# The second layer's gate and value products by Strassen's seven-product form

## The chip, the cores and the metric

The kernel runs on one core of a Trainium2 chip. Times are device microseconds (us) of that core. TensorE (PE in the rows) multiplies, VectorE (DVE), ScalarE (ACT) and GpSimd (POOL) do the elementwise work, SyncE (SP) starts the transfers. SBUF holds the tiles; PSUM holds the sums of the matmuls in eight banks of 128 x 512 fp32, which ScalarE and VectorE can read and write too.

## What is computed

Three layers follow each other, for 4 x 576 = 2304 tokens of 512 features:

```python
x = softmax(q k^T / 8 + decay, causal) v            # 32 heads of 64; heads side by side give x: 2304 x 512
h = x @ w_in;  x = (h * tanh(softplus(h))) @ w_out  # first layer, 512 -> 2048 -> 512
gate = 1 / (1 + exp(-(x @ w_gate)))                 # second layer, 512 -> 1536
out  = (gate * (x @ w_val)) @ w_out2                # 1536 -> 512
```

The weights come as float64.

## The kernel before

Every fp32 product is made of three fp16 products: an operand is split in a high part and the rest (`scaled` writes the high part, `rest` the low one), and `high*high + high*low + low*high` is accumulated in PSUM. A weight tile of 128 x 512 comes in as float64 by one DMA (`load_w`, L536); three VectorE instructions (L558, L562, L566) make fp32 of it, then high part and rest are written.

**Order of the work.** The instructions are not written in program order. Each piece of work is a Python generator that yields what it wants next (an engine and an estimated duration, a key, a buffer). `Order` (L33) runs them all on estimated clocks and issues, engine by engine, what can start first, by due time among those ready. A wrong estimate changes no result, only the order on the five engines. `AFTER` is the estimated delay between the end of an instruction and the start of another that needs it. Every engine then works through its own list in order and waits at the head of it.

**First layer.** Steps of 256 tokens by 256 hidden features (72 of them). `h_stream` makes x @ w_in in a PSUM tile, `mish` puts the activation through ScalarE and VectorE into `g` (L827, L833, L837), `y_stream` multiplies with w_out some steps later, `y_out` writes the new x (`xt`) back in its high and low parts (L919, L921).

**Second layer.** Blocks of 512 tokens (`XB`: four of 512, the last of 256) by steps of 128 hidden features, 60 steps. `gv_stream` (L957 to L978) makes, for each step, the gate in one PSUM tile and the value in another: for each, 4 parts of the 512 input features x 3 matmuls, each with 512 token columns (256 in the last block): 24 matmuls a step. `glu` (L981) takes the gate through ScalarE's tanh (L989), multiplies with the value on VectorE (L992) and splits the result into `zz`. `o_stream` (L1005) multiplies `zz` with w_out2 (3 matmuls of 512 columns for each 128 tokens of a step) and accumulates over the 12 steps of a block in four PSUM tiles; `store` writes them out. `w2_stream` (L934) starts the 36 loads of these weights, spread over the steps of the first layer from step 56 on.

Of the kernel before, what the change touches and what calls it, by code (L numbers as in the profile page):

```python
# [7 lines left out]
FP32 = mybir.dt.float32  # L8
FP16 = mybir.dt.float16
BF16 = mybir.dt.bfloat16  # L10
I32 = mybir.dt.int32
# [13 lines left out]
S_VL = 2.0 ** 4  # L25
# [4 lines left out]
S_Z = S_Y * S_VL * 2.0  # L30
# [21 lines left out]
class Order:  # L52
# [29 lines left out]
    def spawn(self, gen, due):  # L82
        self.n += 1
        t = {"time": self.cur["time"] if self.cur else 0.0, "due": due, "n": self.n, "gen": gen}
        self.step(t, None)

    def step(self, t, value):
        outer, self.cur = self.cur, t
        last = t.get("req", ("",))[0]
# [5 lines left out]
        if r and last == r[0] == "PE":  # L95
            t["time"] -= self.AFTER["PE"]
        if r is None:
            return
        if r[0] in self.ops:
            self.ops[r[0]].append(t)  # L100
        else:
            self.blocked.append(t)
            self.changed = True

# [3 lines left out]
    def done(self, *keys):  # L108
        for k in keys:
            self.event[k] = self.cur["time"]  # L110
        self.changed = True

    def give(self, tag, i):
        self.freed[tag][i] = self.cur["time"]
        self.changed = True

    def pick(self, *plans):

        now, due = self.cur["time"], self.cur["due"]
# [82 lines left out]
    def run(self):  # L202
        while True:
# [29 lines left out]
            if dma:  # L233
# [6 lines left out]
                else:  # L240
                    t["time"] = end
            else:
# [30 lines left out]
def attention_moe_moe_kernel(ctx, tc, qk, v, f, rows_q, rows_k, w_in, w_out, w_gate, w_val, w_out2, out):  # L273
# [26 lines left out]
        "d": 2, "r": 2, "g": 4, "pq": 2,  # L300
        "sp": 4, "pp": 3, "pt": 5, "stage": 4, "vt": 4, "sm": 6, "low": 2, "q": NQ,
        "wr": 3, "wf": 2, "wr2": 2, "wf2": 2,
# [69 lines left out]
    def decay():  # L372
# [3 lines left out]
        zt = mt.tile([128, 768], FP32, tag="pq", name="zt", bufs=BUFS["pq"])[0:NH, 0:S + 1]  # L376
        yield from take("pq")
# [24 lines left out]
        give("pq", 0)  # L402
# [133 lines left out]
    def load_w(hi, lo, src, scale, pool, key, n):  # L536
        wr, wf = ("wr", "wf") if pool is at else ("wr2", "wf2")
        if pool is at:

            yield from need(*(((("st", NPB - 1),),) + (("rq", "rk"),) * n)[n])  # L540
        (ri,) = yield from take(wr, turn=(wr, n))
        if pool is at:

            raw = words(xt[2 + (ri % 3 == 0)], ri % 3 // 2 * 2048, 2048).bitcast(I32)
            raw = raw.rearrange("p (n t) -> p n t", t=2)
        else:
            raw = pool.tile([128, 512, 2], I32, tag="wr", name="wraw", bufs=2)
        yield "SP", 0.5, 128 * 4096
        nc.sync.dma_start(
            out=raw.rearrange("p n t -> p (n t)").rearrange("p (a n) -> p a n", a=src.shape[1]), in_=src  # L550
        )
        (fi,) = yield from take(wf, turn=(wf, n))
        if pool is at:
            w = words(xt[4], fi % 2 * 1024, 1024).bitcast(I32)
        else:
            w = pool.tile([128, 512], I32, tag="wf", name="wf", bufs=2)
# [12 lines left out]
        give(wr, ri)  # L569
# [5 lines left out]
        give(wf, fi)  # L575
        done(key)

    def cols(t, w64, g, scale, pool, key):
# [3 lines left out]
                t[:, 0, k:k + 2], t[:, 1, k:k + 2], src[:, k:k + 2], scale, pool, ("w", key, g, k // 2), n  # L582
# [4 lines left out]
    def rows(t, w64, g, scale, pool, key):  # L587
# [4 lines left out]
                scale, pool, ("w", key, g, a), n,  # L592
# [249 lines left out]
    def h_stream():  # L842
        for i, (blk, g) in enumerate(steps1):
# [10 lines left out]
            for ff in range(2):  # L854
                dst = hp[:, ff * 256:ff * 256 + 256]
                for k in range(KD):
# [9 lines left out]
                    nc.tensor.matmul(dst, lhsT=wl, rhs=xh, start=False, stop=(k == KD - 1))  # L866
            spawn(mish(i, hp, tag, hi), i - MISH)
        done("h")

    def y_stream():  # L870
        for i, (blk, g) in enumerate(steps1):
# [8 lines left out]
            for dm in range(4):  # L880
# [17 lines left out]
                if end and dm % 2:  # L898
                    spawn(y_out(blk, half, acc, ai, g), -100)
            give("g", gi)  # L900
# [26 lines left out]
    w2, z_t = {}, {}  # L927
    W2DUE = 10
    W2BEG = 56
    W2GAP = 0.6  # L930
    NF2 = F2 // 128
    steps = [(blk, fi) for blk in range(len(XB)) for fi in range(NF2)]

    def w2_stream():  # L934
# [229 lines left out]
```

## Time and profile before

| | us |
|---|---|
| median of 3 runs (lowest, highest) | 977.32 (976.13, 978.79) |
| the profiled execution | 978.56 |
| its span, first to last instruction | 976.8 |
| TensorE busy | 914.6 (94%) |
| VectorE busy | 533.0 (55%) |
| ScalarE busy | 464.2 (48%) |
| GpSimd busy | 70.0 (7%) |
| mean granted TensorE clock | 0.993 of full speed |

The busy time of an engine is the union of its instructions' times. A matmul's record is longer than its share of the engine, since matmuls overlap: the time between the starts of two neighbours is what one costs when nothing waits. The chain that ended last is 84% TensorE.

### The profile page before, as it was taken

To read this page: it belongs to the slowest core of one execution; us is meant where nothing else is said; L and a number is where in the kernel's file an instruction comes from. 1 tells how busy PE (TensorE), PEld (TensorE's weight loads), DVE (VectorE), ACT (ScalarE), POOL (GpSimd) and SP (SyncE) were. 2 spreads that over 40 slices of the span, in tenths; PEclk is the share of its full clock that TensorE was granted. 3 is DMA by queue.
4 is the path that set the end of the run, shared out by engine and by line. 5 is a ranking of instruction groups with operands and counts; after the bars stand their busy time and mean duration, and the time that the engine had idled before them with its cause. 6 is when DMAs were issued, how large, how long until landed. Compare 5 with 4: busy or idle time off the path is not lost.

```text
span 976.8 us, 18268 instructions
## 1 busy us (share of the span) xinstructions
PE 914.6 (94%) x7368; PEld 608.9 (62%) x7368; DVE 533.0 (55%) x1262; ACT 464.2 (48%) x912; POOL 70.0 (7%) x74
## 2 busy tenths in 40 slices
PE   2377789999999999999999999999999999999998
PEld 1255568778888888788888744444444444444576
DVE  8998979875656647664888872222222222222232
ACT  8678769898787868886444431110001000100011
POOL 0211301112111102010000000000000000000000
PEclk9998999999999999999999999999999999999999
DMA  7697997668447745545455540010001000100010
GB/s 235 161 212 185 222 229 196 135 133 165 109 102 136 141 98 118 113 78 98 150 161 152 163 130 0 1 44 1 1 1 44 1 0 1 44 1 1 5 40 22
DMA packets 153546, 93.43 MB, mean 96 GB/s; under 512 B 109578, under 2 KB 135242, under 8 KB 153456
## 3 DMA queue, kind: packets, MB, share of 16 engines
q1 hardware_dynamic: 153462, 92.27, 39.2%
q8 instruction: 57, 0.93, 0.4%
q14 instruction: 27, 0.22, 0.1%
HBM read 50.71 MB, written 4.83 MB: 57 GB/s over the span
## 4 chain that ended last, share of the span: by engine, by line
PE 84%; DVE 9%; DMA 3%; issue 1%; SPq 1%; ACT 1%; POOL 0%; DVEq 0%; ACTq 0%; POOLq 0%
PE gv_ps L975 10%; PE gv_ps L976 10%; PE gv_ps L977 10%; PE y_ps L895 6%; PE y_ps L896 6%; PE y_ps L897 6%; PE h_ps L864 6%; PE h_ps L866 5%; PE h_ps L865 5%; PE o_acc L1025 5%; PE o_acc L1023 5%; PE o_acc L1024 5%; PE o_ps L775 3%; DVE pp L437 2%; PE s_ps L657 1%; PE s_ps L658 1%
## 5 line engine op out<-in xcount | busy, mean ns | idle before, releaser
L992 DVE SCALAR_TENSOR_TENSOR z<-t,gv_ps 128x512 f32<-128x512 f32 (+1 forms) x60 | 38.0, 634 | 286.6 <-PE gv_ps L977 250.1
L989 ACT ACTIVATE t<-gv_ps 128x512 f32<-128x512 f32 (+1 forms) x60 | 33.2, 553 | 285.3 <-PE gv_ps L977 276.7
L864 PE MATMUL h_ps<-xt,win 128*128 128x256 f16 x576 | 159.2, 276 | 4.8 <-DVE g L837 3.7
L895 PE MATMUL y_ps<-g,wout 128*128 128x256 f16 x576 | 158.9, 276 | 4.7 <-ACT wout L418 4.7
L896 PE MATMUL y_ps<-g,wout 128*128 128x256 f16 x576 | 158.5, 275 | 3.9 <-DVE wout L437 3.0
L865 PE MATMUL h_ps<-xt,win 128*128 128x256 f16 x576 | 158.8, 276 | 3.1 <-DVE xt L799 2.9
L866 PE MATMUL h_ps<-xt,win 128*128 128x256 f16 x576 | 159.0, 276 | 0.0
L897 PE MATMUL y_ps<-g,wout 128*128 128x256 f16 x576 | 158.5, 275 | 0.0
L605 DVE CUSTOM_DVE_ANT_0 sp<-s_ps,mask 128x384 f32<-128x384 f32 (+4 forms) x144 | 67.3, 494 | 36.9 <-PE s_ps L658 33.9
L976 PE MATMUL gv_ps<-xt,wg 128*128 128x512 f16 (+1 forms) x240 | 85.9, 358 | 0.0
L975 PE MATMUL gv_ps<-xt,wg 128*128 128x512 f16 (+1 forms) x240 | 85.9, 358 | 0.0
L977 PE MATMUL gv_ps<-xt,wg 128*128 128x512 f16 (+1 forms) x240 | 85.9, 358 | 0.0
L977 PE MATMUL gv_ps<-xt,wv 128*128 128x512 f16 (+1 forms) x240 | 85.9, 358 | 0.0
L975 PE MATMUL gv_ps<-xt,wv 128*128 128x512 f16 (+1 forms) x240 | 85.8, 358 | 0.0
L976 PE MATMUL gv_ps<-xt,wv 128*128 128x512 f16 (+1 forms) x240 | 85.8, 358 | 0.0
L437 DVE SCALAR_TENSOR_TENSOR pp<-sp,sm,pp 128x512 f16<-128x512 f32 (+4 forms) x120 | 75.1, 644 | 16.2 <-ACT pp L418 13.6
L1023 PE MATMUL o_acc<-wo,zz 128*128 128x512 f16 x216 | 81.9, 379 | 0.0
L1024 PE MATMUL o_acc<-wo,zz 128*128 128x512 f16 x216 | 81.9, 379 | 0.0
L1025 PE MATMUL o_acc<-wo,zz 128*128 128x512 f16 x216 | 81.9, 379 | 0.0
L673 ACT ACTIVATE sp<-sp,sm 128x384 f32<-128x384 f32 (+3 forms) x112 | 63.8, 570 | 19.6 <-DVE sm L605 19.1
L864 PEld LDWEIGHTS <-win 128*128 128x128 f16 x576 | 56.8, 99 | 18.1 <-issue 3.2
L418 ACT ACTIVATE pp<-sp,sm 128x384 f16<-128x384 f32 (+4 forms) x108 | 63.9, 608 | 8.0 <-DVE sm L630 3.3
(116 smaller groups left out, 1528.9 us busy)
## 6 DMA issues: line engine op xcount, KB each, us to landing
xt<-w_in SPq DMA_DIRECT2D x16, 512.0 KB
xt<-w_out SPq DMA_DIRECT2D x16, 512.0 KB
wraw<-w_gate SPq DMA_DIRECT2D x12, 512.0 KB
wraw<-w_val SPq DMA_DIRECT2D x12, 512.0 KB
wraw<-w_out SPq DMA_DIRECT2D x12, 512.0 KB
st<-qk SPq DMA_DIRECT2D x16, 320.0 KB
out<-ob SPq DMA_DIRECT2D x18, 256.0 KB
st<-qk SPq DMA_DIRECT2D x16, 256.0 KB
```

What stands on the lines that cost most here:

```text
L864: nc.tensor.matmul(dst, lhsT=wh, rhs=xh, start=(k == 0), stop=False)
L865: nc.tensor.matmul(dst, lhsT=wh, rhs=xl, start=False, stop=False)
L866: nc.tensor.matmul(dst, lhsT=wl, rhs=xh, start=False, stop=(k == KD - 1))
L895: nc.tensor.matmul(dst, lhsT=wh, rhs=gh, start=first, stop=False, skip_group_check=True)
L896: nc.tensor.matmul(dst, lhsT=wl, rhs=gh, start=False, stop=False, skip_group_check=True)
L897: nc.tensor.matmul(dst, lhsT=wh, rhs=gl, start=False, stop=last, skip_group_check=True)
L975: nc.tensor.matmul(dst, lhsT=wh, rhs=x[:, 0, k, :], start=(k == 0), stop=False)
L976: nc.tensor.matmul(dst, lhsT=wh, rhs=x[:, 1, k, :], start=False, stop=False)
L977: nc.tensor.matmul(dst, lhsT=wl, rhs=x[:, 0, k, :], start=False, stop=(k == KD - 1))
L1023: nc.tensor.matmul(dst, lhsT=zh, rhs=w[:, 0, ff, :], start=(fi == 0), stop=False)
L1024: nc.tensor.matmul(dst, lhsT=zh, rhs=w[:, 1, ff, :], start=False, stop=False)
L1025: nc.tensor.matmul(dst, lhsT=zl, rhs=w[:, 0, ff, :], start=False, stop=(fi == NF2 - 1))
```

## The change

**The product.** Two hidden steps (256 features) of a block now make one unit: 30 units, named u, of a block and a group j of 0 to 5. The 2 x 2 form is: x cut into token halves (first index) and feature halves (second index), A11, A12, A21, A22; the weights cut by feature halves of the input (rows) and into gate and value (columns): B11, B21 the gate's halves, B12, B22 the value's. Instead of eight products there are seven, in Winograd's arrangement with sums of x (`s`, made by `sums`) and sums of weights (`t1` to `t4`, made by `group`). Each product is 12 matmuls with half a block of columns (256, or 128 in the last block), where before a unit had 96/2 = 48 matmuls with a whole block of columns.

**The sums after the product.** Four PSUM banks A, B, C, D hold the running sums. After a product, ScalarE copies one bank to another (`copy`), and the next product accumulates onto the copy. In one unit TensorE does: b11 in A; t3 in D; t2 onto A; b21 onto B; t1 onto A; t4 onto C; b22 onto D. ScalarE copies A to B after b11, D to an SBUF tile e after t3, A to C after t2, A to D after t1. B is then the gate of the first token half, D its value; C + e is the gate of the second half, A + e its value, both added by VectorE. The output matmuls of the unit before stand in four slots between the products (`some`): after t3, b21, t4 and b22.

**The weights.** Each group takes six loads and three float64-to-fp32 instructions for each as before, then four sums and nine splits (before: six splits). Groups 0 to 2 have tiles of their own, groups 3 to 5 lie in the tiles of the first layer's weights that are free by then. The loads are no longer spread over steps by key; they start as buffers come free once attention is over.

**The order.** `Order` no longer adds the delay `AFTER` between two TensorE requests of one generator when there is a buffer or a key between them; it only adds it where another engine follows. This changes the order from the first layer's steps on. `zt`, a start-up tile, moves into an unused weight tile.

```diff
     def step(self, t, value):
         outer, self.cur = self.cur, t
-        last = t.get("req", ("",))[0]
...
-        if r and last == r[0] == "PE":
-            t["time"] -= self.AFTER["PE"]
...
         if r[0] in self.ops:
+            if r[0] != "PE":
+                t["time"] += t["lag"]
+            t["lag"] = 0.0
...
+            elif e == "PE":
+
+                t["time"], t["lag"] = end, self.AFTER[e]
...
+    def group(j, pool, n, where):
...
+        spawn(pair(w2["b11", j], f2[g1][0], S, ("w", "b11", j)), due)
+        yield from need(v1, ("w", "b11", j))
+        w_g1, w_v1 = f2[g1][0], f2[v1][0]
+        yield from mixed(w_g1, w_v1, w_g1)
+        split("t1", g1, S)
+        yield from need(v2)
+        w_v2 = f2[v2][0]
+        split("b22", v2, S_VL)
+        yield from add(w_v1, w_v2, w_v1, ALU.subtract, 512)
+        split("t3", v1, S_VL)
...
+        yield from mixed(w_v2, w_v2, w_g1)
...
+        split("t2", v2, S)
...
+        split("b21", g2, S)
...
+        yield from add(w_g2, w_g2, w_v2, ALU.subtract, 512)
...
+        split("t4", g2, S)
...
+    def sums(blk):
...
+        for q, fi in zip(("21", "22", "11", "12"), fis):
...
+            yield from add(w.rearrange("p (k n) -> p k n", k=2), part[0], part[1], ALU.add, n)
...
+                yield from add(f["22"][0], f["21"][0], f["22"][0], ALU.add, n)
+                spawn(s_pair(s[0], f["22"][0], n, ("s", blk, 1)), due)
...
+    def product(bank, piece, j, x, half, start):
...
+        for ff in range(2):
+            dst = bank[:, ff * half:ff * half + half]
+            yield "PE", t_pe(6, half)
+            for k in range(2):
...
+                nc.tensor.matmul(dst, lhsT=wh, rhs=xh[:, k], start=first, stop=False, skip_group_check=True)
+                nc.tensor.matmul(dst, lhsT=wh, rhs=xl[:, k], start=False, stop=False, skip_group_check=True)
+                nc.tensor.matmul(dst, lhsT=wl, rhs=xh[:, k], start=False, stop=last, skip_group_check=True)
+
+    def copy(dst, src, first, key):
+        yield from need(*first)
+        yield "ACT", t_act(dst.shape[1], 0.05)
+        nc.scalar.activation(out=dst, in_=src, func=ACTF.Copy)
+        done(key)
 
     def gv_stream():
         yield from need("h")
...
+        yield from take("h", "h", "h", "o")
+        banks = [t_ps(tag, f"bank{i}") for i, tag in enumerate(("h", "h", "h", "o"))]
+
+        yield "PE", t_pe(2, 512)
+        for t in banks[1:3]:
+            nc.tensor.matmul(t, lhsT=xt[0][:, 0, 0, 0:128], rhs=xt[0][:, 0, 1, :], start=True, stop=True)
...
+            yield from need(("v", u - 1), ("ad", u - 1))
+            yield from product(A, "b11", j, q["11"], half, True)
+            spawn(copy(B, A, [("t", u - 1)], ("ab", u)), -100)
+            yield from need(("z", u - 1), ("s", blk, 3))
+            yield from product(D, "t3", j, s[2], half, True)
...
+            spawn(copy(e, D, [], ("de", u)), -100)
+            yield from some(0)
+            yield from need(("ab", u), ("s", blk, 2))
+            yield from product(A, "t2", j, s[1], half, False)
+            spawn(copy(C, A, [("g", u - 1)], ("ac", u)), -100)
+            yield from product(B, "b21", j, q["12"], half, False)
...
+            yield from some(1)
+            yield from need(("ac", u), ("s", blk, 1))
+            yield from product(A, "t1", j, s[0], half, False)
+            spawn(copy(D, A, [("de", u)], ("ad", u)), -100)
...
+            yield from product(C, "t4", j, q["22"], half, False)
...
+            yield from some(2)
+            yield from need(("ad", u), ("s", blk, 4))
+            yield from product(D, "b22", j, s[3], half, False)
...
+    def second(u, v2, ri, C, e, ei, n):
...
+        nc.vector.tensor_tensor(e, C, e, op=ALU.add)
...
+        nc.scalar.activation(out=e, in_=e, func=ACTF.Tanh, scale=0.5 / (S_Y * S_GT))
...
+        nc.vector.scalar_tensor_tensor(v2, e, 1.0, v2, op0=ALU.add, op1=ALU.mult)
```

Where the instructions now stand is shown at three places. On TensorE, the first product of the second layer and what stands ahead of it, before (`gv_ps`, tile 8057; `y_ps` 7810 is the first layer's last block, with g of step 68):

```order
L896 MATMUL y_ps_7810<-g_7868,wout4_88 128x256
L897 LDWEIGHTS wout4_88
L897 MATMUL y_ps_7810<-g_7868,wout4_88 128x256
L975 LDWEIGHTS wg0_7020
L975 MATMUL gv_ps_8057<-xt0_71,wg0_7020 128x512
```

and now (`bank0` is A; `y_ps` with `g_7958` belongs to step 69; the y products of steps 70 and 71 stand behind the whole first unit):

```order
L899 MATMUL y_ps_7832<-g_7958,wout5_89 128x256
L900 LDWEIGHTS wout5_89
L900 MATMUL y_ps_7832<-g_7958,wout5_89 128x256
L1131 LDWEIGHTS b11_0_7018
L1131 MATMUL bank0_8125<-xt0_71,b11_0_7018 128x256
```

The second layer began after step 68's last y product and was mixed with the rest of them; it now begins after step 69's, with one product of 12 matmuls, and bank A is the PSUM tile that the last h step used.

On VectorE, the last g of the first layer (step 71) and what follows, before:

```order
L837 SCALAR_TENSOR_TENSOR g_8067<-h_ps_7992,g_8067 128x512
L437 SCALAR_TENSOR_TENSOR wg4_7031<-wf_8010,wg4_7031 128x512
L558 TENSOR_SCALAR wf_8059<-wraw_8037 128x512
L562 SCALAR_TENSOR_TENSOR wf_8059<-wraw_8037,wf_8059 128x512
L566 SCALAR_TENSOR_TENSOR wf_8059<-wraw_8037,wf_8059 128x512
```

and now:

```order
L838 SCALAR_TENSOR_TENSOR g_8092<-h_ps_8017,g_8092 128x512
L952 TENSOR_TENSOR wf_8006<-wf_8052,wf_8006 128x512
L544 TENSOR_SCALAR wf_8084<-wraw_8072 128x512
L958 SCALAR_TENSOR_TENSOR wout0_84<-wf_8052,wout0_84 128x512
L548 SCALAR_TENSOR_TENSOR wf_8084<-wraw_8072,wf_8084 128x512
L1052 SCALAR_TENSOR_TENSOR wf_8052<-wf_8052,wf_7970 128x512
L552 SCALAR_TENSOR_TENSOR wf_8084<-wraw_8072,wf_8084 128x512
```

Before, this g stood behind 24 of the 36 loads; now it stands behind 21, with their sums and splits (group 3's pieces go to `wout0`), and 16 instructions for group 3's weights stand between it and the first unit's own first VectorE instruction.

On ScalarE, the second layer once its weights are there, before (each step a tanh, and some of the splits):

```order
L989 ACTIVATE t_8595<-gv_ps_8549 128x512
L418 ACTIVATE zz_8606<-z_8596 128x512
L989 ACTIVATE t_8637<-gv_ps_8597 128x512
L418 ACTIVATE zz_8648<-z_8638 128x512
L989 ACTIVATE t_8685<-gv_ps_8639 128x512
```

and now, one whole unit (8125 to 8128 are A to D):

```order
L1138 ACTIVATE bank1_8126<-bank0_8125 128x512
L1138 ACTIVATE e_9297<-bank3_8128 128x512
L1138 ACTIVATE bank2_8127<-bank0_8125 128x512
L1215 ACTIVATE t1_9331<-bank1_8126 128x512
L1138 ACTIVATE bank3_8128<-bank0_8125 128x512
L1238 ACTIVATE e_9297<-e_9297 128x512
L424 ACTIVATE zz_9383<-v2_9352 128x512
L424 ACTIVATE zz_9399<-t1_9331 128x512
```

ScalarE's work, until now behind TensorE's, stands between its products: the copy that the next product accumulates onto is at the head of its list at the time it is wanted.

## Rows read from the trace of the kernel before

**Rows 1.** Stretches: length, busy us (instructions) PE, PEld, DVE, ACT, POOL; PE clock, DMA share, GB/s.
```profile
0.00:150.00 150.00, 93.77 (x922) 68.20 (x923) 132.21 (x324) 112.08 (x233) 25.44 (x28) 0.95 0.84 211
150.00:461.30 311.30, 309.02 (x3521) 254.28 (x3519) 205.67 (x604) 257.42 (x517) 40.77 (x43) 1.00 0.60 121
461.30:544.70 83.40, 83.40 (x766) 74.75 (x765) 68.70 (x117) 35.77 (x61) 1.39 (x1) 1.00 0.53 159
544.70:640.00 95.30, 95.30 (x481) 46.90 (x480) 45.89 (x73) 22.25 (x36) 2.37 (x2) 1.00 0.20 61
640.00:938.00 298.00, 298.00 (x1428) 139.64 (x1427) 70.27 (x120) 32.47 (x56) 0.00 (x0) 1.00 0.04 15
938.00:976.80 38.80, 35.14 (x260) 25.15 (x257) 10.27 (x27) 4.26 (x10) 0.00 (x0) 1.00 0.04 14
```

**Rows 2.** TensorE's waits from 150 us on: total, times, longest.
```profile
PE h_ps L864 <- DVE g L837: 1.6, 1, 1.6
PE s_ps L716 <- DVE sm L605: 0.7, 1, 0.7
```

**Rows 3.** TensorE, 512 columns: start, duration; the first and the thirteenth of a run.
```profile
599.65 0.38 PE L975 MATMUL gv_ps<-xt,wv 128*128 128x512 f16 x1
...
602.24 0.38 PE L1023 MATMUL o_acc<-wo,zz 128*128 128x512 f16 x1
```

**Rows 4.** TensorE, 256 columns, last block: the first and the eighteenth of a run.
```profile
952.76 0.27 PE L975 MATMUL gv_ps<-xt,wg 128*128 128x256 f16 x1
...
954.61 0.27 PE L977 MATMUL gv_ps<-xt,wv 128*128 128x256 f16 x1
```

**Rows 5.** TensorE, 128 columns at full clock, among the scores of attention.
```profile
131.11 0.22 PE L657 MATMUL s_ps<-ma,sa 128*128 128x128 f16 x1
...
131.34 0.27 PE L864 MATMUL h_ps<-xt,win 128*128 128x256 f16 x1
```

**Rows 6.** ScalarE groups by form: instructions, busy us, mean ns, idle before.
```profile
L827 ACT ACTIVATE h_ps<-h_ps 128x512 f32<-128x512 f32 x72 | 41.8, 585 | 28.6 <-PE h_ps L866 28.1
L989 ACT ACTIVATE t<-gv_ps 128x256 f32<-128x256 f32 x12 | 4.6, 383 | 35.6 <-PE gv_ps L977 29.5 <-DMA out<-ob 3.1 <-DVE zz L437 3.0
```

**Rows 7.** A hand-over from TensorE to ScalarE in the last block.
```profile
968.96 0.27 PE L977 MATMUL gv_ps<-xt,wg 128*128 128x256 f16 x1
...
969.27 0.38 ACT L989 ACTIVATE t<-gv_ps 128x256 f32<-128x256 f32 x1 [3.53 <-PE gv_ps L977]
```

**Rows 8.** A hand-over from ScalarE to TensorE, early in the first layer.
```profile
51.86 0.38 ACT L796 ACTIVATE xt<-o_ps 128x256 f16<-128x256 f32 x1 [0.49 <-PE o_ps L775]
...
52.29 0.37 PE L864 MATMUL h_ps<-xt,win 128*128 128x256 f16 x1 [0.48 <-ACT xt L796]
```

**Rows 9.** VectorE on the weights of the second layer: start, duration.
```profile
481.72 0.68 DVE L437 SCALAR_TENSOR_TENSOR wg<-wf,wg 128x512 f16<-128x512 f32 x1
482.32 0.42 DVE L558 TENSOR_SCALAR wf<-wraw 128x512 int32<-128x512 int32 x1
482.78 0.69 DVE L562 SCALAR_TENSOR_TENSOR wf<-wraw,wf 128x512 int32<-128x512 int32 x1
483.50 0.69 DVE L566 SCALAR_TENSOR_TENSOR wf<-wraw,wf 128x512 int32<-128x512 int32 x1
```

**Rows 10.** VectorE: attention's last instruction, and the last g (step 71).
```profile
461.31 0.56 DVE L799 SCALAR_TENSOR_TENSOR xt<-o_ps,xt 128x64 f16<-128x64 f32 x2 [2.06 <-ACT xt L796]
...
544.00 0.69 DVE L837 SCALAR_TENSOR_TENSOR g<-h_ps,g 128x512 f16<-128x512 f32 x1 [0.73 <-ACT g L833]
```

**Rows 11.** GpSimd and VectorE at once.
```profile
524.92 1.39 POOL L446 TENSOR_TENSOR wg<-wf,wg 128x512 f16<-128x512 f32 x1 [76.90 <-ACT wf L442]
...
525.34 1.52 DVE L562 SCALAR_TENSOR_TENSOR wf<-wraw,wf 128x512 int32<-128x512 int32 x1
```

**Rows 12.** TensorE: the last matmul of step 71's h.
```profile
542.44 0.27 PE L866 MATMUL h_ps<-xt,win 128*128 128x256 f16 x1
```

**Rows 13.** A stretch after waits: PE, PEld, DVE, ACT, POOL busy, clock, DMA share, GB/s.
```profile
84.30:86.50 2.20, 2.12 (x11) 1.50 (x12) 2.20 (x7) 2.19 (x5) 0.00 (x0) 0.50 0.99 235
```

**Rows 14.** TensorE around that stretch, 256 columns.
```profile
83.39 0.28 PE L895 MATMUL y_ps<-g,wout 128*128 128x256 f16 x1 [2.22 <-ACT wout L418]
84.38 0.40 PE L896 MATMUL y_ps<-g,wout 128*128 128x256 f16 x1 [0.71 <-DVE wout L437]
...
84.78 0.42 PE L895 MATMUL y_ps<-g,wout 128*128 128x256 f16 x1
...
87.13 0.42 PE L897 MATMUL y_ps<-g,wout 128*128 128x256 f16 x1
```

More of the change, by code (lines that the diff above doesn't have):

```diff
@@ L103, in step, with now @@
             self.changed = True
+    def now(self):
+        return self.cur["time"] + self.cur["lag"] if self.cur else 0.0
     def due(self, x):
@@ L375, in decay @@
         c16 = words(win[NG1 - 2], 0, 3 * S).rearrange("p (a s) -> p a s", a=3)[0:NH]
-        zt = mt.tile([128, 768], FP32, tag="pq", name="zt", bufs=BUFS["pq"])[0:NH, 0:S + 1]
-        yield from take("pq")
+        zt = words(wout[0], 0, 2 * S + 2).bitcast(FP32)[0:NH]
         yield "SP", 0.5, 74000
@@ L531, in prep_v, with float32 @@
         done(("v", i))
[L536 to L556, printed above, removed]
+    def float32(w, raw):
         yield "DVE", 0.335, "port"
@@ new lines, in w2_stream, with place @@
+        free = {}
+        def place(name):
+            t, key = spare.pop(0)
+            free[name] = key
+            return t
+        n = 0
+        NEW = 3
+        for j in range(NJ):
+            for c in PIECES:
+                if j < NEW:
+                    w2[c, j] = pool.tile([128, 2, 512], FP16, name=f"{c}_{j}")
+                else:
+                    w2[c, j] = place((c, j))
+            if j < NEW:
+                o = pool.tile([128, 2, 2, DM], FP16, name=f"wo{j}")
+                w2["o", j] = [o[:, :, a] for a in range(2)]
+            else:
+                w2["o", j] = [place(("o", j)) for a in range(2)]
@@ L981, in glu @@
-    def glu(j, gate, val):
-        n = XB[steps[j][0]]
-        (gp, gtag, gpi), (vp, vtag, vpi) = gate, val
-        di, ri = yield from take("d", "r", turn=("glu", j))
-        t = t_d(n, "t")
-        z = t_r(n, "z")
-        yield "ACT", t_act(n, 0.05), "exp"
-        nc.scalar.activation(out=t, in_=gp, func=ACTF.Tanh, scale=0.5 / (S_Y * S_GT))
-        give(gtag, gpi)
+        yield from take("h", "h", "h", "o")
+        banks = [t_ps(tag, f"bank{i}") for i, tag in enumerate(("h", "h", "h", "o"))]
@@ new lines, in gv_stream, with tanh, value2, first @@
+        for part in outs:
+            yield from part()
+    def tanh(u, t1, B):
+        yield "ACT", t_act(t1.shape[1], 0.05), "exp"
+        nc.scalar.activation(out=t1, in_=B, func=ACTF.Tanh, scale=0.5 / (S_Y * S_GT))
+        done(("t", u))
+    def value2(u, v2, A, e):
+        yield from need(("de", u))
+        yield "DVE", t_dve(v2.shape[1])
+        nc.vector.tensor_tensor(v2, A, e, op=ALU.add)
+        done(("v", u))
+    def first(u, t1, di, D, n):
+        yield from need(("t", u))
```

327 lines of the change are left out of this document (232 added, 95 removed).

## Prediction, made before the changed kernel was run

> **What bounds the kernel now.** I read the page's busy line, then stretches of the span, then TensorE's waits, then neighbouring rows. The stretches [rows 1] show TensorE full from 150 us on: 309.02 of 311.30 us, then 83.40 of 83.40, 95.30 of 95.30 and 298.00 of 298.00. Its waits after 150 us come to 2.3 us, all in attention and the first layer [rows 2]. So the second layer, which begins at about 545 us, costs what its matmuls cost, and each matmul taken out shortens the span as long as nothing new makes TensorE wait. What must be watched is VectorE: 68.70 of the 83.40 us before the second layer, 45.89 of the next 95.30, 70.27 of the 298.00 after that [rows 1]. The second layer's weights are prepared in the first two of these stretches, and there the change adds VectorE work. ScalarE is at 35.77, 22.25 and 32.47 us there and has room.
>
> **What the product saves.** Starts of neighbours give the price of a matmul: 512 columns (602.24 - 599.65)/12 = 0.2158 us [rows 3], 256 columns (954.61 - 952.76)/17 = 0.1088 us [rows 4], 128 columns (131.34 - 131.11)/4 = 0.0575 us [rows 5].
> A unit of a full block had 48 matmuls of 512 columns, 10.36 us; it gets 7 x 12 = 84 of 256, 9.14 us: 1.22 less, and 24 such units give 29.3 us. In the last block 48 of 256 columns, 5.22 us, become 84 of 128, 4.83 us: 0.39 less, 2.4 us for six units. The output matmuls stay 648 of 512 columns. Two matmuls of 512 that first mark banks B and C cost 0.4. TensorE's work falls by 31.3 us.
>
> **The bank copies.** In each unit three products wait for a ScalarE copy (t2, t1, b22). No copy from bank to bank of this kind stands in the trace; the nearest is ScalarE's activation of the h tile in place, 585 ns for 512 columns, and 383 ns for a tanh of 256 out of PSUM [rows 6]. TensorE to ScalarE costs 0.04 us after the matmul's end (969.27 against 968.96 + 0.27) [rows 7], ScalarE to TensorE 0.05 (52.29 against 52.24) [rows 8]. With b11's last matmul starting at 1.20 us of a unit, A is copied by 1.20 + 0.27 + 0.04 + 0.59 + 0.05 = 2.15 us. t2 stands after b11, t3 and one output slot (6 x 0.2158 = 1.29), at 3.91: 1.8 us of cover. The other two copies have a product and a slot between too, 2.60 us in all against 0.85. Unit 0 has no slots, but even there t2 comes at 2.61 against 2.15. The cover is gone only if ScalarE is more than about 1.7 us behind its list; there are eight instructions of about 0.6 us in a unit of 14.3 us (9.14 + 4 x 1.29).
> The last block is tight: in five of its six units two output slots are empty, and t2 and t1 stand one product of 0.69 us behind the one copied. The copy is there at 0.63 + 0.22 + 0.04 + 0.38 + 0.05 = 1.32 us, the next product wants it at 1.38. If ScalarE is at that moment in a split of 0.4 us, 0.4 is lost, at two places in five units: 0 to 4 us, and I take 1, since two or three splits in a unit can hit.
> VectorE's parts (value and gate sums, two products with tanh, two splits) are 6 to 8 instructions, about 5 us of a unit's 14.3; bank D's product is wanted back a slot and a product (2.6 us) after b22, for one VectorE instruction of 0.69. That is covered.
>
> **The weights, and the step into the second layer.** A load's three VectorE instructions start 0.46, 0.72 and 0.60 us apart, 1.78 us in all; any other of 512 columns takes 0.60 [rows 9]. Between attention's last instruction and the last g [rows 10] stood 114: 24 loads and 42 others, 24 x 1.78 + 42 x 0.60 = 67.9 us, which is the row's 68.70. Now there are 132: 21 loads and 69 others (16 g, 4 outputs of the first layer, and 49 splits and sums for weights and for block 0's x): 78.8 us. That last g matters more than it did, because bank A is step 71's h tile: b11 cannot start until VectorE has read it. Step 71's last matmul is at 542.44 [rows 12]; then two steps of y (48 x 0.1088 = 5.2) and the two marking matmuls come, so A is wanted at 548.2, 86.3 us after attention's last instruction ends at 461.9. The work fills 91% of that. Five sums lie on GpSimd in this stretch. In the one collision in the rows, VectorE's instruction of 0.69 took 1.52 while GpSimd's ran [rows 11]: 0.83 each, 4.2 us. That leaves 3.3 us for waits; VectorE had 15 us of them in the stretch before (83.40 - 67.9), most for things that TensorE's pace sets and that come in time. If none of these cost anything here, A is not late; if all return, it is late by 78.8 + 15.5 + 4.2 - 86.3 = 12 us. I take 2, near the lower end, because a longer list has more work to put into the gaps. ScalarE's first copy (A to B) stands behind two splits of group 3's t2 and b21, whose sources VectorE finishes some 4 us after that g; it is the same lateness, not another.
> After it, up to the sums of block 1's x, VectorE has 115 instructions: 15 loads and 70 others, 68.7 us, and 5.8 for seven collisions with GpSimd. TensorE needs 5.2 (y of steps 70, 71) + 9.1 + 5 x 14.3 + 1.3 = 87 us until it wants those sums. VectorE is at 86% there, but each unit's own sums stand behind weights in its list: 0 to 5 us, taken as 1, for the same reason.
> On these GpSimd sums the Trainium skill (SBUF — State Buffer, "SBUF: two separate sides") says that VectorE with two SBUF inputs and a GpSimd instruction that reads SBUF exclude each other for the whole of the one that came first. By that a collision could cost up to GpSimd's 1.39 us, and twelve 16.7 instead of 10.0. The row agrees: VectorE's instruction ended 0.55 us after GpSimd's.
>
> **The order.** The list on TensorE differs from the first h steps on. Up to 150 us TensorE works 93.77 us [rows 1], so 56 us of waiting are open to a better or worse order; from there to 461 it can only lose. VectorE is at 132.21 and ScalarE at 112.08 of the 150 us, and this work is the same, so I bound the effect by 5 us either way, about a tenth of that waiting, and take 0.
>
> **The sum.** -29.3 - 2.4 + 0.4 + 1 + 2 + 1 + 0 = -27.3. From the profiled execution's 978.56 that is 951.3; its median lies 1.24 lower (977.32), so 950.0. The kernel's end is as long as before: two tiles to write out after the last output matmul.
>
> **Rivals.**
> A: VectorE sets the pace from 461 to 640 us. For it: 91% and 86%, lists in order, and collisions priced from one row. Against: both stretches have room and TensorE has other work up to 548. At its bounds, 12 and 5 instead of 2 and 1, it is 14 us dearer: 964. Chance 0.15.
> B: the order helps and every wait is hidden: -31.3 - 5 = -36 from the median, 941. For it: 56 us of early waiting. Against: VectorE and ScalarE, not TensorE's order, are full there. Chance 0.12.
> C, slower: the copies are not covered. In every full unit, t2, t1 and b22 would each wait for the whole hand-over of 0.85 us and one ScalarE instruction ahead of it (0.6): 3 x 1.45 = 4.4 us a unit, 104 for 24, less the 31: 1050. It decides from 1.3 us a unit on (31.3/24). Against: 1.8 us of cover at each place, ScalarE at half load. Chance 0.04.
> D: TensorE's clock falls. After waits of 2.22 and 0.71 us in the first layer the granted clock was 0.50 of full speed, the lower level of 1.2 GHz [rows 13], and a matmul of 256 columns cost (87.13 - 84.78)/11 = 0.214 us instead of 0.109 [rows 14]. If a twelfth of the second layer's 390 us of work ran so, 32 us would be lost and the saving gone, 977; with a sixth 1009. Against: the waits that I find in a full unit are none, and about 0.2 us in the last block. Chance 0.04, half of it slower than before. In the Trainium skill, TensorE: Matmul & The Clock Gate, "A second HAM failure mode: psum-queue depth-cycling", says that cycling through PSUM banks with small idle gaps makes this clock swing between its levels; the trace of before has no such cycling with gaps, so no row bears on it.
> My forecast, 942 to 957, has the remaining 0.65.
>
> **Range and chances.** 942 to 963 leaves out most of B's far end, C and D, and takes in A and the 5 us of the order: about 0.8. About 0.3% (3 us) is what a measurement here can tell from no change. Slower: C, and half of D, 0.06. Same: 0.02, from D's middle. Faster: 0.92.
>
> **What would show it.** Right: the matmuls of the second layer 0.109 us apart, units of 14.3 us from block 1 on without a wait of TensorE for ScalarE or VectorE, and the last block's units near 7.4 us (4.83 + 2 x 1.29). Waits on bank A of up to some 5 us at 545 to 560 us, for VectorE's last g or the first copy. VectorE over 85% from 461 to 600. Wrong: waits of TensorE for copies in each unit (C), a granted clock under 1.00 after 560 us (D), a second layer that begins more than 5 us before or after 548 because attention ends elsewhere (order), or VectorE waits that sum to over 10 us by unit 6 (A).

## The result and the profile after

| | before | changed |
|---|---|---|
| median | 978.06 us (976.13 to 978.85, 4 runs) | 951.75 us (951.48 to 952.80, 4 runs) |
| ratio, 95% interval | | 0.9741 [0.9726, 0.9756] |
| profiled execution, its span | 978.56, 976.8 | 951.72, 949.9 |

One execution of all those in this document, of the kernel "planner told, two steps" below, ran at a mean granted clock of 0.759 and took 1179.47 us; its median is of the other five.

The page of the changed kernel, its busy line (engine, busy us, share of the span, instructions):

```profile
PE 881.4 (93%) x8450; PEld 695.0 (73%) x8450; DVE 614.0 (65%) x1374; ACT 568.0 (60%) x1108; POOL 83.5 (9%) x82
```

Its stretches, columns as in [rows 1], which they answer:

```profile
0.00:150.00 150.00, 93.44 (x938) 69.51 (x939) 133.38 (x320) 110.49 (x230) 24.91 (x27) 0.97 0.81 208
150.00:455.00 305.00, 300.13 (x3402) 248.48 (x3401) 206.51 (x602) 252.76 (x517) 35.97 (x40) 0.99 0.63 124
455.00:540.00 85.00, 85.00 (x821) 75.86 (x819) 75.77 (x126) 40.55 (x71) 6.76 (x5) 1.00 0.41 129
540.00:640.00 100.00, 96.77 (x765) 74.62 (x763) 85.95 (x136) 51.41 (x87) 13.13 (x8) 1.00 0.26 85
640.00:910.00 270.00, 270.00 (x2099) 199.21 (x2097) 98.65 (x158) 99.43 (x173) 2.74 (x2) 1.00 0.05 17
```

TensorE is full from 640 us to the tail (35.00 of 35.00 from 910 to 945), at a granted clock of 1.00, as it was before. In the long stretch ScalarE does 99 us in 270 where it did 32 in 298, VectorE 99 where it did 70. The only idle time of the second layer lies between 540 and 640.

TensorE's waits from 150 us on (who waited for whom: total, times, longest; the last row is the second layer's whole account), beside [rows 2]:

```profile
PE s_ps L658 <- DVE sm L606: 2.1, 2, 1.4
...
PE bank L1131 <- ACT bank L1138: 3.2, 3, 1.2
```

The copy of D to SBUF comes once in each unit, so its starts give the units' lengths. ScalarE, start and duration; two neighbours in a full block, then two in the last block:

```profile
641.51 0.60 ACT L1138 ACTIVATE e<-bank 128x512 f32<-128x512 f32 x1 [0.67 <-PE bank L1133]
655.86 0.60 ACT L1138 ACTIVATE e<-bank 128x512 f32<-128x512 f32 x1 [0.73 <-PE bank L1133]
...
915.68 0.38 ACT L1138 ACTIVATE e<-bank 128x256 f32<-128x256 f32 x1 [0.24 <-PE bank L1133]
922.97 0.38 ACT L1138 ACTIVATE e<-bank 128x256 f32<-128x256 f32 x1 [0.24 <-PE bank L1133]
```

A full unit takes 14.35 us, and 18 in a row from 627.16 to 885.46 take 14.35 each. A unit of the last block takes 7.28 or 7.29. Of the full units only the three after 580.40 are clearly longer, 16.84, 15.23 and 14.69.

**Where 26.84 us of profiled time went.** Attention's last VectorE instruction ends 0.60 later than in [rows 10] (461.91 + 0.56), and step 71's last h matmul as much later than in [rows 12] (543.04). From there to the end of the last output matmul it was 430.70 us and is 403.00, 27.70 less. The tail behind it is 0.20 longer, the time around the span 0.06. Of the 27.70, units without waits give 24 x (10.36 - 9.17) = 28.6 and 6 x (5.22 - 4.69) = 3.2, where 9.17 is 14.35 less 24 x 0.2158, and 4.69 is 7.28 less 12 x 0.2158; the marking matmuls take 0.4 and the waits 3.7, by which the three longer units exceed 14.35. (The rows' 3.2 count each wait from the end of a matmul's record of 0.38 us, 0.16 after that matmul's own 0.2158; the waits cost what lies between the starts.) That is 27.7, and nothing is left over.

**The three waits.** GpSimd, VectorE and ScalarE of the changed kernel, start and duration:

```profile
578.35 1.42 POOL L452 TENSOR_TENSOR zz<-v,zz 128x512 f16<-128x512 f32 x1 [15.85 <-ACT v L448]
579.72 1.33 POOL L452 TENSOR_TENSOR zz<-t,zz 128x512 f16<-128x512 f32 x1
581.02 1.71 POOL L952 TENSOR_TENSOR wf<-wf 128x512 f32<-128x512 f32 x1
...
578.66 1.38 DVE L544 TENSOR_SCALAR wf<-wraw 128x512 int32<-128x512 int32 x1
580.08 1.53 DVE L548 SCALAR_TENSOR_TENSOR wf<-wraw,wf 128x512 int32<-128x512 int32 x1
581.53 1.49 DVE L544 TENSOR_SCALAR wf<-wraw 128x512 int32<-128x512 int32 x1
...
583.65 0.63 ACT L424 ACTIVATE win<-wf 128x512 f16<-128x512 f32 x1 [2.65 <-DVE wf L552]
...
586.18 0.58 ACT L1138 ACTIVATE bank<-bank 128x512 f32<-128x512 f32 x1
...
586.81 0.27 PE L1131 MATMUL bank<-s,t 128*128 128x256 f16 x1 [1.24 <-ACT bank L1138]
```

Beside three GpSimd instructions in a row, three of VectorE take 1.38, 1.53 and 1.49 us instead of the 0.42, 0.69 and 0.42 of [rows 9]: 2.9 us lost. ScalarE's list holds two splits of a later group ahead of the copy that this unit waits for (the second starts at 585.64). Both splits wait for VectorE, so the copy of 586.18 is late though its own source, a bank, was ready, and TensorE waits 1.24 us for it. The second wait (0.93 at 591.82) comes out of lists that are still late: the copy of 591.18 stands behind VectorE's value sum of 590.40, and that sum behind loads of which two had waited for their DMA (0.43 and 0.28). How much of this wait is the collision's is not shown apart. The third (1.06 at 621.74) is a collision again: a GpSimd sum of 1.54 at 618.32 stretches VectorE's next split to 1.65, and the value sum and the copy behind it are late.

### The profile page after: what moved, and what is told of

The parts are those of the page before. It is cut to its first block, busy times and chain, and to the rows that moved or that the text cites. A ratio compares the mean times of both kernels' runs of the same rounds, so it can differ in the third digit from the quotient of the medians.

```text
span 949.9 us, 20753 instructions
## 1 busy us (share of the span) xinstructions
PE 881.4 (93%) x8450; PEld 695.0 (73%) x8450; DVE 614.0 (65%) x1374; ACT 568.0 (60%) x1108; POOL 83.5 (9%) x82
## 4 chain that ended last, share of the span: by engine, by line
PE 64%; DVE 4%; DMA 0%; POOL 0%; ACT 0%; issue 0%; ACTq 0%; POOLq 0%
PE bank L1131 8%; PE bank L1133 8%; PE bank L1132 8%; PE o_acc L1279 4%; PE o_acc L1278 4%; PE o_acc L1277 4%; PE y_ps L898 4%; PE y_ps L900 4%; PE y_ps L899 4%; PE h_ps L865 4%; PE h_ps L867 4%; PE h_ps L866 4%; PE o_ps L776 2%; PE s_ps L658 1%; PE s_ps L659 1%; PE s_ps L717 1%
## 5 line engine op out<-in xcount | busy, mean ns | idle before, releaser
L1221 DVE TENSOR_TENSOR v<-bank,e 128x512 f32<-128x512 f32 (+1 forms) x30 | 19.1, 637 | 169.2 <-ACT bank L1138 169.2
L1138 ACT ACTIVATE bank<-bank 128x512 f32<-128x512 f32 (+1 forms) x90 | 48.5, 539 | 93.0 <-PE bank L1133 90.3
L443 DVE SCALAR_TENSOR_TENSOR pp<-sp,sm,pp 128x384 f16<-128x384 f32 (+4 forms) x122 | 78.7, 659 | 17.8 <-ACT pp L424 16.4
L424 ACT ACTIVATE pp<-sp,sm 128x384 f16<-128x384 f32 (+4 forms) x115 | 66.2, 599 | 11.1 <-issue 3.8
L865 PEld LDWEIGHTS <-win 128*128 128x128 f16 x576 | 56.9, 99 | 16.6 <-issue 3.4
L898 PEld LDWEIGHTS <-wout 128*128 128x128 f16 x576 | 56.8, 99 | 13.9 <-ACT wout L424 4.2
L867 PEld LDWEIGHTS <-win 128*128 128x128 f16 x576 | 56.9, 99 | 12.0 <-issue 3.9
L899 PEld LDWEIGHTS <-wout 128*128 128x128 f16 x576 | 56.9, 99 | 11.9 <-DVE wout L443 2.3
L866 PEld LDWEIGHTS <-win 128*128 128x128 f16 x576 | 57.0, 99 | 10.7 <-issue 1.7
L776 PE MATMUL o_ps<-pt,vt 128*64 128x128 f16 (+1 forms) x1440 | 48.8, 218 | 16.7 <-DMA pt<-pp 14.9
L776 PEld LDWEIGHTS <-vt 128*64 128x64 f16 x1440 | 39.9, 114 | 31.4 <-issue 21.3
L658 PE MATMUL s_ps<-ma,sa 128*128 128x128 f16 (+3 forms) x128 | 39.1, 322 | 25.0 <-DVE sm L606 12.7
L900 PEld LDWEIGHTS <-wout 128*128 128x128 f16 x576 | 56.9, 99 | 7.1
L838 DVE SCALAR_TENSOR_TENSOR g<-h_ps,g 128x512 f16<-128x512 f32 x72 | 49.0, 684 | 18.8 <-ACT g L834 18.5
```

The lines of the kernel that those rows point to most:

```text
L443: nc.vector.scalar_tensor_tensor(dst, a, scale, b, op0=ALU.mult, op1=ALU.subtract)
L776: nc.tensor.matmul(o_ps[64 * hh:64 * hh + 64, col:col + n], lhsT=vv[:, jc, vl, 64 * hh:64 * hh + 64], rhs=ptt[:, k, q0:q0 + n], start=(jc ...
L865: nc.tensor.matmul(dst, lhsT=wh, rhs=xh, start=(k == 0), stop=False)
L866: nc.tensor.matmul(dst, lhsT=wh, rhs=xl, start=False, stop=False)
L898: nc.tensor.matmul(dst, lhsT=wh, rhs=gh, start=first, stop=False, skip_group_check=True)
L899: nc.tensor.matmul(dst, lhsT=wl, rhs=gh, start=False, stop=False, skip_group_check=True)
```

## The experiments

| kernel | median us | ratio to before, 95% interval |
|---|---|---|
| order alone | 979.24 | 1.0031 [1.0020, 1.0042] |
| changed, old estimate | 955.20 | 0.9774 [0.9758, 0.9790] |
| changed, no GpSimd in the second layer | 948.92 | 0.9711 [0.9698, 0.9724] |
| changed, copies twice | 958.57 | 0.9820 [0.9803, 0.9837] |
| changed, copies four times | 1028.71 | 1.0537 [1.0506, 1.0568] |
| before, half columns | 980.57 | 1.0040 [1.0025, 1.0055] |
| changed, an eighth product | 993.38 | 1.0165 [1.0144, 1.0186] |
| no GpSimd, estimate switched | 946.18 | 0.9688 [0.9671, 0.9704] |
| no GpSimd, old estimate | 950.91 | 0.9724 [0.9705, 0.9744] |
| changed, 21.6 us more on VectorE | 975.54 | 0.9992 [0.9981, 1.0003] |
| the same, planner told, two steps | 959.10 | 0.9822 [0.9800, 0.9845] |
| the same, planner told, one step | 954.78 | 0.9773 [0.9759, 0.9786] |

The kernel before, run beside them, had medians of 976.2 to 976.8, so kernels are compared by ratio. The differences from the changed kernel that the text gives are of medians (from 951.75); by ratio they come out up to 0.9 us more or less.

**The gain is the product left out.** First the price of half the columns:

```
-  nc.tensor.matmul(dst, lhsT=wh, rhs=x[:, 0, k, :], ...)      # and its two neighbours
+  for c in (slice(0, cols_ // 2), slice(cols_ // 2, cols_)):
+      nc.tensor.matmul(dst[:, c], lhsT=wh, rhs=x[:, 0, k, c], ...)
```

> The kernel before, each gate and value matmul of the second layer split into two of half the columns (96 of 256 instead of 48 of 512 in a full unit); nothing else. By the spacing of neighbours, 24 x (96 x 0.1088 - 48 x 0.2158) = 2.1 us and 6 x (96 x 0.0558 - 48 x 0.1088) = 0.8: 980 to 982, ratio 1.002 to 1.005. Rival (a narrower matmul costs more than its spacing among neighbours says, since each brings a weight load of its own): 0.01 us more for each of 2880 matmuls, 29 us, 1010.

Measured 1.0040, some 2.4 to 5.4 us; expected 2.9. TensorE's neighbours there, start and duration, with a weight load each:

```profile
703.27 0.27 PE L979 MATMUL gv_ps<-xt,wg 128*128 128x256 f16 x1
703.38 0.27 PE L980 MATMUL gv_ps<-xt,wg 128*128 128x256 f16 x1
```

They stand 0.11 apart, the spacing of [rows 4]; the rival is out. Then the eighth product, put back:

```
   yield from product(B, "b21", j, q["12"], half, False)
+  yield from product(B, "b21", j, q["12"], half, False)
```

> The changed kernel with an eighth product: b21's twelve matmuls run twice in each unit (the gate gets that product twice). Theory (the whole gain is the product that is left out): 24 x 12 x 0.1088 + 6 x 12 x 0.0558 = 31.3 + 4.0 = 35.4, less up to 3.2 for the waits at 580 to 600 us that it gives time for: 984 to 987, so slower than before by 0.6 to 0.9%. Rival (part of the gain is that products, sums and outputs interleave better than the old pairs did): 975 or less, with units that grow by less than 1.31 us.

Its units are 15.66 us (14.35 + 1.31) and 7.95 (7.28 + 0.67), to the hundredth the sum of the theory, and the kernel is slower than before by 1.4 to 1.9%. Most of the 6 to 9 us beyond the forecast lie at one place, a unit of 24.59 us from 601.43 on; 2.0 more in the profile are a later end of attention. Its waits in the second layer:

```profile
PE bank L1131 <- ACT bank L1138: 6.5, 1, 6.5
```

and the stretches at that wait and behind it (the granted clock is the third number from the end):

```profile
608.30:612.00 3.70, 0.00 (x0) 0.00 (x0) 3.60 (x8) 0.77 (x2) 0.00 (x0) 1.00 0.01 2
612.00:616.00 4.00, 1.66 (x8) 1.13 (x8) 4.00 (x7) 2.74 (x5) 1.58 (x1) 0.54 0.02 4
```

Again a copy stood behind splits, the first of which had waited 3.50 us for VectorE:

```profile
612.57 0.63 ACT L424 ACTIVATE wout<-wf 128x512 f16<-128x512 f32 x1 [3.50 <-DVE wf L552]
...
613.71 0.58 ACT L1138 ACTIVATE bank<-bank 128x512 f32<-128x512 f32 x1
```

After this longer wait the granted clock was at its lower level (0.54), and matmuls of 256 columns stood 0.21 us apart. The waits of 1.24 us and less in the changed kernel left it at 1.00.

**The cover of the copies.** Each ScalarE copy was issued twice, then four times, without telling the planner, so the order stayed:

```
-  nc.scalar.activation(out=dst, in_=src, func=ACTF.Copy)
+  for _ in range(2):      # 4 in the second run
+      nc.scalar.activation(out=dst, in_=src, func=ACTF.Copy)
```

> The changed kernel with each ScalarE copy of a bank done twice in a row (0.58 us more ahead of each product that accumulates onto it, 0.37 in the last block), order unchanged. Theory (1.8 us of cover in a full unit, 0.06 in the last block): full units stay at 14.35 us; in the last block t2 and t1 of five units each wait 0.3 us: +3; with a little more at 575 to 600 us, 954 to 957. Rival (the copies are on the path, only short): +0.58 at three places of 24 units, 42 us, and 6 in the last block: about 1000.

Twice: ScalarE in a full unit (where the copies of D to SBUF are 14.35 us apart as before) and, below, in the last block:

```profile
805.04 1.20 ACT L1139 ACTIVATE bank<-bank 128x512 f32<-128x512 f32 x2 [1.38 <-PE bank L1133]
...
936.69 0.77 ACT L1139 ACTIVATE bank<-bank 128x256 f32<-128x256 f32 x2 [0.21 <-PE bank L1133]
```

TensorE's waits there from 640 us on:

```profile
PE bank L1131 <- ACT bank L1139: 1.9, 10, 0.2
```

958.57 is 1.6 over the forecast. Full units did not move. In the last block a unit went from 7.28 to 7.97: two places, each 0.40 more copy less the 0.06 of cover, 0.34. Five such units are 3.4 of the 6.8 us; 1.9 are in the units before 640, where copies already stood behind splits, and about 1.2 is a later end of attention, whose order is the same.

> The changed kernel with each ScalarE copy of a bank done four times in a row (1.75 us more ahead of each product that accumulates onto it, 1.1 in the last block), order unchanged. Cover theory: 2.15 + 1.75 = 3.90 us against the 3.91 at which t2 wants its bank, and 0.85 + 1.75 = 2.60 against 2.60 for t1 and b22, so the cover is just used up; ScalarE is then busy 12.3 of 14.35 us, and a copy that stands behind a tanh or a split is late by 0 to 0.6 us: units of 14.4 to 16.2 us. Last block: 1.05 us at two places of five units, +10.5. Together 965 to 1010. Rival (more cover than I counted, up to a whole unit): full units stay at 14.35 and only the last block is longer, 962 to 966.

Four times missed the forecast by 19 us, and the rival too. ScalarE there, a full unit:

```profile
766.58 0.62 ACT L424 ACTIVATE wout<-af 128x512 f16<-128x512 f32 x1
767.10 0.59 ACT L1293 ACTIVATE ob<-o_acc 128x512 f32<-128x512 f32 x1
767.57 0.63 ACT L424 ACTIVATE win<-af 128x512 f16<-128x512 f32 x1
768.10 2.44 ACT L1139 ACTIVATE bank<-bank 128x512 f32<-128x512 f32 x4
```

I had allowed one instruction ahead of a copy; here three stand there, 1.5 us. Units are 15.28 to 20.53 us. The shortest show a copy that I had left out: the edit makes four of the copy of D to SBUF too (2.48 us for 0.60), and it stands directly ahead of A to C. In the unit from 699.77 on, with no split or store between these copies, t2 loses only 0.07 us, as the sum of cover said, and t1 waits 0.65 for A to C. So what stands ahead of a copy in ScalarE's list uses the cover up as the copy does. Units of the last block are 10.43 us where about 9.4 was forecast, and after waits of 3.15, 2.40 and 2.96 us the granted clock was 0.50 to 0.53 for some 4 to 6 us each, which was not in the forecast either.

**The order.** First the new estimate without Strassen's form, then that form without the new estimate:

```
-  t["time"] = end + self.AFTER[e]        # also for TensorE, taken back if TensorE follows
+  t["time"], t["lag"] = end, self.AFTER[e]   # for TensorE: added only if another engine follows
```

> The kernel before with the re-estimated order alone (a matmul product that follows another on TensorE no longer waits out the 0.2 us in the planner); all of its arithmetic is as before. Theory (the order is worth nothing, the removed product everything): 978 +- 2 us, ratio to before 0.998 to 1.002. Rival (part of the gain is the order's): 966 to 975, TensorE's idle time in the first 455 us (56 + 2 us before) smaller by as much.

> The changed kernel with the old estimate of TensorE's order, Strassen's form kept. Theory: 951.7 +- 3, whatever moves lies in the first 150 us; attention ends within 3 us of the changed kernel's. Rival (the order carries part of the gain): 955 to 965. A third: the old estimate costs in the second layer, where its products would be mixed otherwise: units longer than 14.35 us after 640 us.

Neither main theory held to its bound. In the old form the new estimate costs 0.2 to 0.4%; in the changed form it gives 3.4 us. The place explains the signs: with the old estimate attention's last VectorE instruction starts at 459.37 us, with the new one at 461.91, 2.5 later. One such pair could be chance, since two profiles with the old estimate, of the kernel before and of its half columns, are 3.9 apart (461.31 and 457.42). But all five profiles with the old estimate until attention is done lie from 457.42 to 461.31, and all nine with the new one from 461.78 to 464.44. Behind it, the waits of the second layer with the old estimate are:

```profile
PE o_acc L1272 <- POOL zz L445: 3.4, 1, 3.4
PE bank L1124 <- DVE t L1220: 2.2, 2, 1.2
PE bank L1124 <- ACT bank L1131: 1.7, 2, 1.0
```

That is 7.3 us against 3.2, or 8.1 against 3.7 between starts. The longest is followed by a lower granted clock, which costs 1.7 us more:

```profile
600.00:604.00 4.00, 4.00 (x20) 2.60 (x19) 2.85 (x6) 2.38 (x5) 1.38 (x1) 0.57 0.07 27
```

So the old estimate wins 2.5 us ahead of 462 and loses about 6 behind it.

**GpSimd.** The sums, splits and z of the second layer without it:

```
-  (plan,) = pick([("DVE", t_dve(n), "port")], [("POOL", t_pool(n))])
-  yield plan
-  (nc.vector if plan[0] == "DVE" else nc.gpsimd).tensor_tensor(out, a, b, op=op)
+  yield "DVE", t_dve(n), "port"
+  nc.vector.tensor_tensor(out, a, b, op=op)      # scaled() and rest() likewise
```

> The changed kernel with no GpSimd instruction in the second layer (sums, splits and z on VectorE or ScalarE; the arithmetic is the same). Theory (three GpSimd instructions in a row stretched VectorE's of 0.42 and 0.69 us to 1.4 to 1.5 and so made the three waits of 3.2 us at 580 to 600): the waits shrink to under 1 us, 948 to 950. Rival (VectorE has too much to do there, GpSimd takes a real share off it): eight GpSimd instructions become 0.6 us each on VectorE, about 5 us more in a stretch of 86 of 100, waits of 3 to 8 us, 952 to 956.

2.8 us faster. VectorE now takes on the z itself, at normal length:

```profile
579.53 0.69 DVE L1249 SCALAR_TENSOR_TENSOR zz<-v,zz 128x512 f16<-128x512 f32 x1
```

and TensorE's waits in the second layer shrink to two, both in unit 0:

```profile
PE bank L1130 <- ACT bank L1137: 0.5, 2, 0.4
```

VectorE is busy 85.2 us between 540 and 640 here (55.51 + 29.64), not more than the 85.95 with GpSimd's help. Two kernels more part this from the order:

```
+  elif e == "PE" and "att" not in self.event:      # old estimate until attention is done
+      t["time"], t["old"] = end + self.AFTER[e], True
```

> The changed kernel with no GpSimd instruction in the second layer and with the old order estimate until attention is done, the new one after. Theory (the old estimate ended attention 2.5 us earlier, 459.4 against 461.9; what made it dearer lay in the second layer's first units alone): 945.5 to 947.5, waits in the second layer under 1.5 us. Rival (an earlier end of attention only makes VectorE later for the second layer's weights, which it prepares at the same pace): 948 to 950, as without GpSimd alone, with the 2.5 us back as waits at 545 to 600.

> The changed kernel with no GpSimd instruction in the second layer and with the old order estimate throughout. Theory (the old estimate's 3.4 us in the changed kernel came from GpSimd alone, 3.4 us of waits on a z from GpSimd and VectorE behind it): as with the estimate switched after attention, 945 to 947. Rival (its order of unit 0 and of the first layer's last products costs by itself): 948 to 951, with waits of 2 to 5 us at 545 to 605.

The switch gives 946.18, the fastest of all: attention's last VectorE instruction at 459.76 and a wait of 0.2 us behind. With the old estimate throughout, the rival held: 950.91, and without any GpSimd the waits are there, now on VectorE itself. TensorE's waits in the second layer of the switched kernel:

```profile
PE bank L1135 <- ACT bank L1142: 0.2, 1, 0.2
```

and of the one with the old estimate throughout:

```profile
PE bank L1123 <- DVE t L1219: 5.0, 3, 1.9
```

**VectorE's room (rival A).** The last of a load's three instructions twice:

```
   yield from float32(w, raw)
+  nc.vector.scalar_tensor_tensor(w, raw[:, :, 0], 29, w, ...)     # the same once more
```

> The changed kernel with the last of a load's three VectorE instructions done twice for all 36 loads of the second layer, order unchanged: 36 x 0.60 = 21.6 us more on VectorE between 462 and 640, some 12.6 of them before the second layer begins (VectorE had 9 us of room there) and 9 in its first units (14 us of room). Theory (room is filled before TensorE waits, rival A's point not reached): waits of about 3 to 10 us, 955 to 962. Rival A's mechanism at once (lists in order, each us more on VectorE is a us of waiting): 971 to 975. No cost at all: 951 to 953.

23.8 us for 21.6: my theory fell, rival A's number came, in part by other ways than rival A's. TensorE's waits from 462 us on:

```profile
PE bank L1134 <- ACT bank L1141: 7.7, 4, 3.4
PE y_ps L898 <- DVE xt L926: 5.8, 1, 5.8
PE bank L1134 <- DVE g L838: 3.2, 1, 3.2
PE bank L1134 <- DVE t L1230: 2.4, 3, 1.6
```

VectorE's list at the first of them, and TensorE after it (start, duration):

```profile
528.79 0.69 DVE L548 SCALAR_TENSOR_TENSOR wf<-wraw,wf 128x512 int32<-128x512 int32 x1
...
530.00 0.68 DVE L926 SCALAR_TENSOR_TENSOR xt<-y_ps,xt 128x512 f16<-128x512 f32 x1
...
530.73 0.37 PE L898 MATMUL y_ps<-g,wout 128*128 128x256 f16 x1 [5.84 <-DVE xt L926]
...
531.11 0.42 PE L900 MATMUL y_ps<-g,wout 128*128 128x256 f16 x1
```

The first layer's own g and y, which stand between the loads, came late, not only the last g. 19.1 us are waits where 3.2 were; after the 5.84 the matmuls stood 0.21 apart for 3 us instead of 0.109. The two profiles are 25.9 us apart: 16.9 are waits (20.6 against 3.7 between starts), about 6 are matmuls at a granted clock of 0.50 after three of the waits (5.84, 3.18 and 2.63 us), and 2.5 are a later end of attention, whose order is the same. So the fixed list made TensorE wait about 0.8 us for each us more on VectorE. Is it VectorE's time or its list? The same work, told to the planner:

> The same 36 extra VectorE instructions (21.6 us) as in the run before, but the planner is told of them (0.6 us each), so it may order VectorE's list anew and give other work to ScalarE and GpSimd. If the 24 us came from a list in fixed order, in which the first layer's g and a unit's own sums stand behind loads grown longer: most of it comes back, 954 to 962. If VectorE's time as such is what is used up between 462 and 640 us (rival A as capacity): 968 to 976 again.

> The same work as in the run before (the last of a load's three VectorE instructions twice, 36 loads, 21.6 us), told to the planner as one step of 1.2 us instead of two of 0.6. If the order of VectorE's list decides (untold 975.5, told in two steps 961.4): 957 to 965 again, with the first layer ending within 3 us of the changed kernel's 543. If the two-step run owed its time to where other instructions slipped in between the two: 968 to 976.

In these two orders part of the second layer works on other values than in the changed kernel, and where they get in I did not find. All instructions are there, but a wait that a right order would need may be missing, so the two times are a hint and no proof. 959.10 and 954.78 (below the 957 forecast): of some 24 us, all but 7 to 8 and 3 came back. In the second, the stretch from 540 us on:

```profile
540.00:640.00 100.00, 94.72 (x746) 72.64 (x744) 96.23 (x157) 50.47 (x87) 9.61 (x7) 1.00 0.31 99
```

VectorE works 96.23 of 100 us and TensorE waits 5.3. Of the 21.6 us, some 10 are in this stretch (the changed kernel has 85.95), 9 in the 30 us behind it and 2 ahead of it. So the first run's loss was for the most part that of a list in fixed order; that VectorE has some 20 us of room in another order is likely, but not shown. The profiles of the two steps and the one are 8.9 us apart: 3.6 of waits, 4.3 of lower clock behind them, 1.1 of attention's end. Why their waits differ is open.

## The prediction, step by step

The forecast was 950.0 us, within 942 to 963; 951.75 was measured. In the profiles the forecast sum of -27.3 came out as -26.84: the product -31.3 (forecast -31.3), copies 0 (+1), waits 3.7 (+3), attention's later end 0.6 (0), the tail and the rest 0.3 (0). So the mechanism held, and misses of about 1 us on both sides cancelled.

- *The product saved, -31.3*: right. Units of 14.35 us for 14.3, 7.28 for 7.4; the last block's matmuls are 4.69/84 = 0.0558 apart, not 0.0575, which is 0.8 us more gain, and the full units' 9.17 for 9.14 takes the same away again. The two experiments on product and columns show the product as the cause.
- *Copies covered, +1*: right, and 0 in the event. A bank's copy takes 582 ns for the 585 I took, 368 for 383. The last block has as little cover as I counted: its copy of 915.07 ends at 915.44, and t2's first matmul is at 915.49, 0.05 later, the hand-over of [rows 8]. Copies twice confirm this cover, and that a full unit has at least 0.58; four times confirm the 1.8 of t2 where nothing stands ahead.

```profile
915.07 0.37 ACT L1138 ACTIVATE bank<-bank 128x256 f32<-128x256 f32 x1 [0.77 <-PE bank L1133]
...
915.49 0.22 PE L1131 MATMUL bank<-s,t 128*128 128x128 f16 x1
```

- *Transition, +2, and units 1 to 4, +1*: the sum was right (3.2 in the rows, 3.7 between starts), its places were not, so the size was luck. Bank A was not late at all: VectorE read it in the g of 545.71, and b11's first matmul starts without a wait at 548.82, forecast 548.2, of which 0.6 is attention's later end. All waits fell in units 2 and 4, mostly for collisions with GpSimd (no GpSimd: 0.5 left, in unit 0).

```profile
545.71 0.69 DVE L838 SCALAR_TENSOR_TENSOR g<-h_ps,g 128x512 f16<-128x512 f32 x1
...
548.82 0.27 PE L1131 MATMUL bank<-xt,b 128*128 128x256 f16 x1
```

- *91% and 86% as room*: the reasoning failed, though its number stood. VectorE was at 77.41 of 81.2 us between 461.9 and 543.1, 95%. In fixed order there was little room (16.9 us more of waits for 21.6 more on VectorE), and in an order made for it perhaps some 20 us. I read a share where the list decides.
- *Order, 0*: wrong as an argument. Measured in the changed form it is worth 3.4 us: 2.5 lost before 462 and about 6 won after it, as waits and as clock. I looked for its effect in the first 150 us alone, and took the rest to be settled by the form.
- *Rivals*: A did not come; as a fixed list it is what a heavier load would have met, as capacity it is likely out. (At its bounds it is 964, just outside the range that was said to take it in.) B did not come; the best version, without GpSimd, reaches 946 where B said 941, half of that step by the order. C begins between copies twice and four times. D did not come in the changed kernel: clock 1.00 from 455 to 945 us. In some variants where TensorE waited longer, its lower clock came.

## What to carry to other kernels

When the engine that sets the end is full, count its instructions, take their spacing among neighbours, and check by putting the removed work back. The cover of a hand-over is what stands between in the waiting engine's list less what stands ahead in the helping engine's; a busy share of 90% says nothing of either. A planner's estimate and a new form of the work should be tried apart and by stage: here one helped in one stage and cost in the other, and switching it between them with one helper engine taken out gave some 5 us more.

## What the runs showed of the hardware

- GpSimd beside VectorE stretches VectorE's one-source conversion as much as its two-source operations: 0.42 to 1.38 and 1.49 us, 0.69 to 1.53. It goes the other way too: with the old estimate a z on GpSimd took 5.09 us instead of some 1.2 to 1.7, while VectorE worked without a gap until 598.74, and TensorE waited 3.39 of them:

```profile
594.62 5.09 POOL L445 TENSOR_TENSOR zz<-v,zz 128x512 f16<-128x512 f32 x1 [24.43 <-ACT v L441]
```

The Trainium skill (SBUF — State Buffer, "SBUF: two separate sides") says that the two engines lock a shared pair of ports for a whole instruction, and that VectorE's fast modes with one source fall under it too, which I had left out of the forecast; the rows agree in both directions.
- A ScalarE copy from one PSUM bank to another is no dearer than into SBUF: 582 against 596 ns for 512 columns.
- Attention's last VectorE instruction started at 461.91 to 464.44 us in eight profiled executions of the changed form with the new estimate, which have one order up to there: a difference of some 2.5 us between single profiles can be of this kind.
- The length of a wait alone did not settle what TensorE's clock did after it. With the old estimate a wait of 3.39 us (at 599.77) was followed by a granted clock of 0.57 over 4 us. With 21.6 us more on VectorE, a wait of 3.39 (at 607.38) was followed by 1.00, and one of 2.63 (at 645.92) by 0.50 over 3.4 us.
